# Retention and two feed-forward layers on one core: a new written order for the first stage, head-pair scores in alternating banks, attention inputs first

## The chip, the core and the metric

One of the eight cores of a Trainium2 chip runs the whole kernel. The metric is the time of one execution on the device, in microseconds (us). Its engines each take their own instructions in order: TensorE (PE in the profile, PEld for its weight loads), VectorE (DVE), ScalarE (ACT), GpSimd (POOL) and SyncE (SP), which here only issues transfers. Matrix results go to eight PSUM banks of 512 floats per partition, called bank 0 to 7 below.

## What is computed

```python
# q, k, v: (4, 8, 576, 64); every array is float32
scores = scale * q @ k.T
Dmat   = where(rel >= 0, gamma[head] ** rel, 0)     # rel = query position - key position
x      = (scores * Dmat) @ v                        # regrouped to 2304 tokens x 512
# layer 1, 512 -> 2048 -> 512, a cubic over a quadratic between its products
h = x @ w_in
g = (a0 + a1*h + a2*h**2 + a3*h**3) / (1 + |b0|*|h| + |b1|*h**2 + 1e-6)
x = g @ w_out
# layer 2, 512 -> 1536 -> 512
xn  = x / sqrt(mean(x*x) + 1e-6) * rms_g
out = (silu(xn @ w_gate) * (xn @ w_val)) @ w_out2
```

## The kernel before

**Attention** runs in 20 chunks, 4 batches of 5; a chunk has 128 positions, the last one of a batch 64. The decay between chunks is carried in a state `S` per head (64 by 64). The four head pairs of a chunk lie side by side in a bank, and the two heads of a pair lie in partitions 0 to 63 and 64 to 127 of the inputs.

**Layer 1** takes 384 tokens at a time (6 tiles) against 16 slices of `w_in` and `w_out`. One such pair of a tile and a slice is a step `s` of 96. Every float32 operand is split in a high and a low part, and three of the four products are made, so that a step has 12 matmuls up (`m1_up`) and 12 down (`m1_down`), of 384 columns each. The down products of a tile add up in banks 0 to 3 (`acc`). Weights arrive as float32 bits and are split by a chain over ACT, DVE and POOL (class `Weights`). **Layer 2** follows with its own weights.

**The first stage** is attention, the 32 weight slices of layer 1 and steps 0 to 17 of layer 1, all mixed. Its order is written out by hand: `PLAN` (L37) is a string of short names that are emitted one by one; `in_order` chains the instructions of each engine in that order, so every engine runs them as they stand and waits where an input is late. From step 18 on (`S0`) a plain loop takes over; the change doesn't touch it. The names that this text uses, with their engine:

| name | what it is | engine |
|---|---|---|
| LQ, LK | load of a chunk's q and k, of its k and v (`load_qk`, `load_kv`) | SP |
| LR | load of a weight slice (`Weights.load`), three buffers | SP |
| CH, CL, WH | weight split on ACT (L173, L180, L201) | ACT |
| CS, CG | weight split on DVE (L184, L191) | DVE |
| CA, WL | weight split, add (L197) and low part (L205) | DVE or POOL |
| PV | v times its decay (`prep_v`, L251) | POOL |
| SC | scores (`att_scores`, L263), one head of each pair, one bank | PE |
| R | scores times the mask (`att_mask`, L273), into one of three buffers | DVE |
| ST, SA | the chunk's own state (L341) and its addition to `S` (L350, L348) | PE, DVE |
| OS, OV | output from the state (L301) and from the chunk (L315) | PE |
| XO | output times its decay, into the one buffer `xe` (L324) | DVE |
| XS | store of `xe` to DRAM (L334) | SP |
| XH, XL | high and low part for the first token tile, chunks 0 to 2 | ACT, DVE |
| U, UU; D, DD | the halves of `m1_up` (L365 to L367); `m1_down` with g high (L374, L375) and low (L378) | PE |
| QQ | a product of the element-wise part (`el_qq`, L408) | POOL |
| PA, PB, NA, NB, NC, GL | other element-wise steps (L412, L416, L432, L436, L441, L451) | DVE |

A number behind a name is the chunk, the weight slice or the step `s`, and behind a slash stands the bank, or `v` and `p` for DVE and POOL. Ahead of `PLAN` five warming matmuls run on PE (L618), and ACT's queue issues the small tables.

Of the kernel before, what the change touches and what calls it, by code (L numbers as in the profile page):

```python
# [42 lines left out]
LQ7 LK7 PV5/p WH4 LR7 UU0 R11 CS5 SC12/4 CF0 BA0 CG5 BU0 CA5/v U1/6 BQ0 LR8 PV6/p PA0 WH5 UU1 R12 QQ0/p PB0
OV5/4 BA1 XO4 WL4/p BU1 SC13/7 LQ8 BQ1 XS4 PA1 PV7/p R13 YA0 YB0 PB1 ST5/7 QQ1/p CH6 SA5 LK8 NA0 CL7 SC14/7
WL5/p NB0 CL8 R14 CH7 CS6 OS6/7 YA1 NC0 YB1 CG6 OV6/0 GH0 NA1 PV8/p D0 LQ9 NB1 CS7 CA6/v LR9 CG7 WH6 GL0/v
WL6/p NC1 U2/5 XO5 GH1 CA7/p UU2 CH8 GL1/v XS5 LR10 CS8 ST6/4 WH7 CG8 SC15/6 LK9 BU2 SA6 CA8/p BA2 DD0 R15 BQ2
OS7/4 PA2 LR11 WL7/p CL9 PB2 SC16/6 WH8 XO6 QQ2/p CH9 OV7/0 R16 XS6 CL10 PV9/p U3/7 LQ10 YA2 CS9 YB2 ST7/6 CG9
CL11 UU3 LK10 SA7 CA9/p NA2 XR0 SC17/6 BA3 XR1 NB2 BU3 LR12 WL8/p D1 R17 BQ3 PA3 WH9 QQ3/p PB3 OS8/6 CH10 NC2
PV10/p OV8/0 YA3 XO7 YB3 CS10 U4/4 LQ11 GH2 CG10 XS7 NA3 CA10/p UU4 CL12 NB3 DD1 GL2/v BU4 LR13 WL9/p NC3
SC18/5 BA4 D2 GH3 R18 PA4 BQ4 PB4 CH11 SC19/5 QQ4/p GL3/v DD2 WH10 R19 ST8/7 YA4 CS11 WL10/p SC20/5 SA8 LK11  # L50
YB4 XO8 CL13 OS9/7 R20 CH12 XS8 U5/6 CG11 SC21/5 CA11/v LR14 CS12 WH11 OV9/0 CG12 UU5 LQ12 LK12 PV11/p NA4 D3
NB4 BA5 CA12/p BU5 R21 BQ5 PA5 OV10/5 LR15 WL11/p NC4 WH12 DD3 LQ13 PB5 CL14 QQ5/p XO10 CH13 SC22/5 XS10 GH4
# [5 lines left out]
WH17 U8/4 CG18 YA7 CA18/v UU8 YB7 LR21 WL17/p NA7 WH18 NB7 BA8 NC7 BU8 PV15/p GL6/v BQ8 WL18/p PA8 OS13/5 CH19
PB8 CL19 DD6 CS19 CH20 CG19 OV13/0 CL20 CS20 LQ16 QQ8/p XO12 GH7 CL21 GL7/v SC28/7 XS12 CA19/p D7 YA8 R28 YB8
LR22 CG20 WH19 U9/6 NA8 CA20/p NB8 SC29/7 NC8 UU9 WL19/p LR23 WH20 R29 GH8 XO13 ST13/7 CH21 WL20/p DD7 SA13  # L60
LK16 XS13 BA9 GL8/v SC30/5 BU9 CS21 CG21 OS14/7 BQ9 OV14/0 R30 CA21/p CH22 SC31/4 LQ17 PA9 CL22 LK17 PB9 U10/5
LR24 QQ9/p WH21 R31 CL23 PV16/p UU10 XO14 YA9 XS14 CS22 OV15/4 BU10 CG22 YB9 SC32/7 LQ18 PA10 CA22/p BA10 NA9
BQ10 D8 R32 LR25 PV17/p WH22 NB9 ST15/7 PB10 QQ10/p CL24 DD8 LK18 SA15 NC9 WL21/p SC33/7 YA10 XO15 YB10 R33
CH23 WL22/p OS16/4 XS15 GH9 NA10 OV16/0 CS23 CH24 CG23 U11/7 CL25 LQ19 CA23/v D9 LR26 CS24 WH23 CG24 NB10
PV18/p UU11 GL9/v CA24/p NC10 SC34/6 BU11 XO16 GH10 DD9 LR27 WL23/p PA11 WH24 XS16 SC35/4 R34 CL26 WL24/p PB11
ST16/6 CH25 SA16 LK19 BA11 R35 U12/6 BQ11 CS25 CH26 QQ11/p GL10/v U13/4 CL27 CG25 SC36/5 YA11 CS26 YB11 UU12
CA25/p R36 NA11 OS17/5 BU12 LR28 CG26 WH25 OV17/0 PV19/p PA12 BA12 PB12 UU13 BQ12 WL25/p NB11 NC11 D10 BU13
# [12 lines left out]
def retention_moe_kernel(  # L80
# [542 lines left out]
    act.activation(out=qb, in_=ones[:, 0:2], func=ACTF.Abs)  # L623
    act.dma_start(out=gv, in_=t_gv)
    act.dma_start(out=cf, in_=coef)
    act.dma_start(out=rg, in_=rms_g)
# [232 lines left out]
```

## Time and profile before

| what | value |
|---|---|
| median of three runs | 988.83 us (986.68 to 989.68) |
| the profiled execution, its own time | 990.85 us |
| its span, first to last instruction | 989.0 us |
| mean granted clock of TensorE | 0.989 |
| PE, PEld busy | 962.4 us (97%), 903.2 us (91%) |
| DVE, ACT, POOL busy | 569.8, 535.3, 325.0 us (58, 54, 33%) |

The profile and the trace are of that one execution; the 1.85 us between its time and its span lie outside the first and last instruction. Records of one engine overlap a little at their ends, and "busy" counts each moment once. A row ends with the idle time before it, and behind an arrow what ended that.

### The profile page before, as it was taken

The page shows a single profiled execution, that of the slowest core. Times are in us where ns is not written, and L with a number is a line of the kernel's source. Part 1 is how long each engine was busy: PE and PEld are TensorE (multiplying, and loading weights), DVE is VectorE, ACT ScalarE, POOL GpSimd, SP SyncE. Part 2 cuts the span into 40 slices and gives each one's busy share as a digit, 9 for nine tenths or more (in the row PEclk, how much of TensorE's full clock was granted, in tenths as well). Part 3 has the DMA queues.
Part 4 walks back from the last instruction along what each step waited for, and adds up shares of the span by engine and source line. Part 5 has one row for each costly group of instructions (what it writes and reads, how often), then busy time and mean ns, then how long its engine had stood idle before and what let it go on. Part 6 is the DMA issues. An engine that isn't in the chain of part 4 may idle for free. (4 is left out here: it accounts for less than half of the span.)

```text
span 989.0 us, 15086 instructions
## 1 busy us (share of the span) xinstructions
PE 962.4 (97%) x5854; PEld 903.2 (91%) x5854; DVE 569.8 (58%) x1022; ACT 535.3 (54%) x1028; POOL 325.0 (33%) x308
## 2 busy tenths in 40 slices
...
GB/s 352 280 239 239 222 271 121 105 1 33 33 1 43 22 32 33 1 33 33 22 75 96 107 155 131 125 112 95 34 1 64 1 1 49 1 1 19 14 1 32
DMA packets 38584, 79.85 MB, mean 81 GB/s; under 512 B 6256, under 2 KB 21744, under 8 KB 38512
## 3 DMA queue, kind: packets, MB, share of 16 engines
...
q8 instruction: 46, 0.75, 0.3%
...
## 5 line engine op out<-in xcount | busy, mean ns | idle before, releaser
L536 PE MATMUL bank<-x,w 128*128 128x384 f32 x528 | 176.8, 336 | 0.6 <-DVE sg L542 0.6
L537 PE MATMUL bank<-x,w 128*128 128x384 f32 x528 | 177.0, 335 | 0.3 <-POOL x L290 0.3
L538 PE MATMUL bank<-x,w 128*128 128x384 f32 x528 | 177.1, 335 | 0.0
L542 DVE TENSOR_TENSOR sg<-sg,bank 128x384 f32<-128x384 f32 x72 | 39.8, 553 | 217.8 <-PE bank L538 212.1
L290 POOL TENSOR_TENSOR x<-xr,x 128x384 fp32r<-128x384 f32 x44 | 47.7, 1099 | 287.1 <-ACT x L286 287.0
L365 PE MATMUL bank<-x,w 128*128 128x384 f32 x384 | 131.8, 343 | 6.9 <-DVE u L416 4.1
L374 PE MATMUL bank<-g,w 128*128 128x384 f32 x384 | 129.9, 340 | 3.0 <-ACT g L447 2.8
L367 PE MATMUL bank<-x,w 128*128 128x384 f32 x384 | 129.0, 336 | 0.0
L366 PE MATMUL bank<-x,w 128*128 128x384 f32 x384 | 128.9, 336 | 0.0
L375 PE MATMUL bank<-g,w 128*128 128x384 f32 x384 | 128.1, 335 | 0.1
L541 ACT ACTIVATE sg<-bank 128x384 f32<-128x384 f32 x72 | 35.4, 491 | 166.5 <-PE bank L538 166.5
L408 POOL TENSOR_TENSOR q<-q,ah 128x384 f32<-128x384 f32 x96 | 99.3, 1034 | 78.8 <-ACT q L395 75.7
L451 POOL TENSOR_TENSOR g<-u,g 128x384 fp32r<-128x384 f32 x80 | 82.3, 1029 | 69.0 <-issue 37.0
L536 PEld LDWEIGHTS bank<-x,w 128*128 128x128 f32 x528 | 99.1, 188 | 4.1 <-DVE sg L542 0.9
L537 PEld LDWEIGHTS bank<-x,w 128*128 128x128 f32 x528 | 99.1, 188 | 3.3 <-POOL x L290 0.7
L538 PEld LDWEIGHTS bank<-x,w 128*128 128x128 f32 x528 | 99.1, 188 | 0.4
L544 ACT ACTIVATE y<-sg 128x384 fp32r<-128x384 f32 x72 | 37.7, 524 | 101.8 <-DVE sg L542 101.8
L378 PE MATMUL bank<-g,w 128*128 128x384 f32 x384 | 86.8, 340 | 0.0
L412 DVE TENSOR_TENSOR u<-u,bank 128x384 f32<-128x384 f32 x96 | 52.9, 551 | 56.6 <-ACT u L401 53.5
L365 PEld LDWEIGHTS bank<-x,w 128*128 128x128 f32 x384 | 72.3, 188 | 11.6 <-DVE u L416 6.2
L374 PEld LDWEIGHTS bank<-g,w 128*128 128x128 f32 x384 | 72.3, 188 | 5.3 <-ACT g L447 4.1
L423 ACT ACTIVATE bank<-q,cst 128x384 f32<-128x384 f32 x96 | 56.0, 583 | 35.3 <-POOL q L408 28.1
...
## 6 DMA issues: line engine op xcount, KB each, us to landing
...
```

The source lines that it names most:

```text
L365: pe.matmul(out=h, lhsT=w[:, 0, ks], rhs=x[:, 0, k], start=(k == 0), stop=False)
L366: pe.matmul(out=h, lhsT=w[:, 0, ks], rhs=x[:, 1, k], start=False, stop=False)
L367: pe.matmul(out=h, lhsT=w[:, 1, ks], rhs=x[:, 0, k], start=False, stop=(k == KD - 1))
L374: pe.matmul(out=acc[m], lhsT=w[:, 0, ms], rhs=g[:, 0], start=(j == 0), stop=False)
L375: pe.matmul(out=acc[m], lhsT=w[:, 1, ms], rhs=g[:, 0], start=False, stop=False)
L378: pe.matmul(out=acc[m], lhsT=w[:, 0, ms], rhs=g[:, 1], start=False, stop=(j == J1 - 1))
L408: eng.tensor_tensor(out=q, in0=q, in1=el_t[i]["ah"], op=ALU.mult)
L423: act.activation(out=el[i], in_=el_t[i]["q"], func=ACTF.Abs_reciprocal_sqrt, bias=cst[:, 0:1])
L451: eng.tensor_tensor(out=g[:, 1], in0=el_t[i]["r"], in1=g[:, 0].bitcast(F32), op=ALU.subtract)
L536: pe.matmul(out=t, lhsT=w[:, 0, ks], rhs=x[:, 0, k], start=(k == 0), stop=False)
L537: pe.matmul(out=t, lhsT=w[:, 0, ks], rhs=x[:, 1, k], start=False, stop=False)
L538: pe.matmul(out=t, lhsT=w[:, 1, ks], rhs=x[:, 0, k], start=False, stop=(k == KD - 1))
```

## The change

- **A pair's scores.** `att_scores` makes both heads of a chunk in one go, into two banks, and takes the heads in turn: head 0 of pair 0, head 1 of pair 0, head 0 of pair 1, and so on. The two heads use different halves of the array's rows. A bank number over 99 gives two banks (`101` is banks 0 and 1).
- **Banks 0 to 3** serve attention too, as the order says; the first D stands behind the last chunk.
- **Masks.** The upper triangle comes into `ones` by a load and is set to 1 after the stage. A 64-position chunk takes one R over 128 partitions instead of two over 64, so there are 36 R instead of 40.
- **Tables.** The decay tables of chunks 1 to 4 of a batch were four loads on SP; now POOL makes them from the first (`make_gq`, 4 instructions). Two small tables go together in `ta`, two others in `cr`.
- **The order.** SP's first load is the first q and k instead of three weight slices. All of attention stands ahead of D0 and of U5; before, U14 stood ahead of the last chunk's outputs. Of the DVE and POOL work, counted in `PLAN`:

| name | before, DVE / POOL | now, DVE / POOL |
|---|---|---|
| PV | 0 / 20 | 9 / 11 |
| CA | 11 / 21 | 11 / 21 |
| WL | 7 / 25 | 13 / 19 |
| QQ | 0 / 18 | 6 / 12 |
| XL | 3 / 0 | 2 / 1 |
| R | 40 / 0 | 36 / 0 |
| GQ | 0 / 0 (four loads) | 0 / 4 |

```diff
 PLAN = """
-LR0 LR1 LR2 LQ0 LK0 LQ1 LK1 LQ2 LK2 GQ1 GQ2 GQ3 CH0 GQ4 CL0 CS0 CG0 CL1 CA0/v CH1 LR3 WH0 CS1 CG1 CL2 WL0/v
...
+LQ0 KC0 LK0 LR0 KG0 LQ1 LK1 LQ2 LK2 SC0/101 LR1 R0 LR2 PV0/p R1 ST0/0 CL0 OV0/1 SA0 CH0 GQ1 XO0 LQ3 GQ2 LK3
...
-    gv = at_p.tile([128, NC, NH, 1], F32, name="gv")
-    msk = at_p.tile([128, 1, CH], F32, name="msk")
+    ta = at_p.tile([128, HD + NC * NH + (NC - 1) * NP], F32, name="ta")
+    msk, msk_h = ones[:, None, :], ta[:, None, 0:HD]
...
-    def load_gq(c):
-        sp.dma_start(out=gq[c], in_=t_gq[c, :, :, 0:size(c)])
-
-    def att_scores(i, e, b):
-        n, ks = keys(i, e)
-        qk, r = qk_b[i % 3], slice(64 * e, 64 * e + 64)
-        sc = banks[b].rearrange("p (n c) -> p n c", n=NP)
+    def load_at():
+        sp.dma_start(out=ones, in_=t_dm)
+        sp.dma_start(out=ta, in_=t_at)
+
+    def make_gq(c):
+        n = size(c)
+        pool.tensor_tensor(
+            out=gq[c][:, :, 0:n], in0=gq[0][:, :, 0:n],
+            in1=gf[:, c - 1].to_broadcast([128, NP, n]), op=ALU.mult,
+        )
+
+    def att_scores(i, b):
+        qk = qk_b[i % 3]
+        for e in range(2):
+            rets[i, e] = banks[(b % 100 // 10 if b > 99 else b, b % 10)[e]].rearrange("p (n c) -> p n c", n=NP)
         for p in range(NP):
-            pe.matmul(
-                out=sc[ks, p, 0:n], lhsT=qk[r, 1, p, 0:n], rhs=qk[r, 0, p, 0:n],
-                start=True, stop=True,
-            )
-        rets[i, e] = sc
+            for e in range(2):
+                n, ks = keys(i, e)
+                r = slice(64 * e, 64 * e + 64)
+                pe.matmul(
+                    out=rets[i, e][ks, p, 0:n], lhsT=qk[r, 1, p, 0:n], rhs=qk[r, 0, p, 0:n],
+                    start=True, stop=True,
+                )
 
     def att_mask(i, e):
-        n, ks = keys(i, e)
+        n = size(steps[i][1])
         sc = rets[i, e]
         rets[i, e] = ret_p.tile([128, NP, CH], F32, tag="ret", name="ret")
+        if n < CH:
+            rets[i, 1] = rets[i, e]
         dve.tensor_tensor(
-            out=rets[i, e][ks, :, 0:n], in0=sc[ks, :, 0:n],
-            in1=msk[ks, :, ks].to_broadcast([n, NP, n]), op=ALU.mult,
+            out=rets[i, e][:, :, 0:n], in0=sc[:, :, 0:n],
+            in1=(msk if n == CH else msk_h).to_broadcast([128, NP, n]), op=ALU.mult,
         )
...
-        "SC": lambda i, a: att_scores(*divmod(i, 2), a),
+        "SC": att_scores,
...
-        "XL": lambda i, a: split_lo(0, *x0(i), dve),
+        "XL": lambda i, a: split_lo(0, *x0(i), a),
```

**The start, on SP.** These are its first transfers before (`raw` is a weight slice, `xb` q and k, `kv_...` k and v, `gq_...` a decay table):

```order
L163 DMA raw<-in_w_in_dram 128x1024 x3
L238 DMA xb<-in_qkT_dram 128x512 x2
L243 DMA kv_109<-in_kv_dram 128x1024
L238 DMA xb<-in_qkT_dram 128x1024
L243 DMA kv_110<-in_kv_dram 128x1024
```

and now:

```order
L237 DMA xb<-in_qkT_dram 128x1024
L255 DMA ones<-in_t_dm_dram 128x128
L256 DMA ta<-in_t_at_dram 128x120
L242 DMA kv_107<-in_kv_dram 128x1024
L163 DMA raw<-in_w_in_dram 128x1024
L649 DMA gq_110<-in_t_gq_dram 128x512
L237 DMA xb<-in_qkT_dram 128x1024
```

The first q and k are ahead of all else; the first weight slice is fifth, the second comes behind three chunks.

**The first scores, on PE.** Before (bank_98 is bank 0, bank_102 bank 4, and so on):

```order
L263 MATMUL bank_102<-xb 128x128 x4
L263 MATMUL bank_103<-xb 128x128 x4
L341 MATMUL bank_104<-kv_109 64x64 x8
L263 MATMUL bank_105<-xb 128x128 x4
L263 MATMUL bank_102<-xb 128x128 x4
L315 MATMUL bank_103<-ret,kv_109 64x128 x8
```

and now, from the third pair of the first chunk on (bank_97 is bank 0, bank_98 bank 1):

```order
L273 MATMUL bank_97<-xb 128x128
L273 MATMUL bank_98<-xb 128x128
L273 MATMUL bank_97<-xb 128x128
L273 MATMUL bank_98<-xb 128x128
L352 MATMUL bank_97<-kv_107 64x64 x8
L326 MATMUL bank_98<-ret,kv_107 64x128 x8
```

Four matmuls of one head in a row have become single ones of the two heads in turn, and the second chunk's scores, which stood ahead of the first chunk's output (L315), now stand behind it.

**The end of the stage, on DVE.** Bank 4 holds step 16, and step 18, the loop's first, waits for it. PB16 is the L416 row of bank_102 before; behind it stand GL14, GL15, PA17 and PB17:

```order
L441 SCALAR_TENSOR_TENSOR bank_104<-u,cf,bank_104 128x384
L416 SCALAR_TENSOR_TENSOR u<-u,cf,bank_102 128x384
L451 TENSOR_TENSOR g<-bank_105,g 128x384
L451 TENSOR_TENSOR g<-bank_104,g 128x384
L412 TENSOR_TENSOR u<-u,bank_103 128x384
L416 SCALAR_TENSOR_TENSOR u<-u,cf,bank_103 128x384
```

Now PB16 is the L427 row of bank_101, and PB17 that of bank_102:

```order
L427 SCALAR_TENSOR_TENSOR u<-u,cr,bank_101 128x384
L462 TENSOR_TENSOR g<-bank_103,g 128x384
L184 TENSOR_SCALAR ft<-ft 128x512
L191 SCALAR_TENSOR_TENSOR ft<-raw,ft 128x512
L443 SCALAR_TENSOR_TENSOR q<-q,bank_104 128x384
L447 SCALAR_TENSOR_TENSOR bank_104<-q,bank_104 128x384
L423 TENSOR_TENSOR u<-u,bank_102 128x384
L452 SCALAR_TENSOR_TENSOR bank_104<-u,cr,bank_104 128x384
L427 SCALAR_TENSOR_TENSOR u<-u,cr,bank_102 128x384
```

Between PB16 and PB17 there were three instructions and are now seven, two of them for the last weight slice. In `PLAN` ten DVE steps stand behind PB16 now, and four did before.

## Rows read from the trace of the kernel before

**Rows 1.** Busy time by stretch: us and instructions of each engine, clock, DMA share, GB/s.

```profile
0.00:187.84 187.84, 171.17 (x1555) 145.64 (x1555) 149.36 (x263) 117.00 (x211) 104.83 (x94) 0.95 0.72 234
9.95:187.84 177.89, 165.09 (x1545) 143.18 (x1545) 145.34 (x254) 111.87 (x203) 104.62 (x90) 0.95 0.72 231
187.84:500.00 312.16, 311.17 (x1771) 308.56 (x1772) 226.65 (x421) 247.76 (x498) 179.37 (x180) 0.99 0.09 28
```

**Rows 2.** Timeline of PE: the first matmul of step 18.

```profile
187.84 0.44 PE L365 MATMUL bank<-x,w 128*128 128x384 f32 x1 [2.62 <-DVE u L416]
```

**Rows 3.** Groups of DVE's instructions up to 187.8 us: busy us, mean ns, idle before.

```profile
L273 DVE TENSOR_TENSOR ret<-bank,msk 128x512 f32<-128x512 f32 x32 | 22.1, 689 | 12.0 <-PE bank L263 10.1 <-PE bank L315 1.6
L205 DVE TENSOR_TENSOR w<-ft,w 128x512 fp32r<-128x512 f32 x7 | 5.9, 854 | 0.0
L412 DVE TENSOR_TENSOR u<-u,bank 128x384 f32<-128x384 f32 x17 | 9.3, 549 | 3.3 <-ACT u L401 3.2
L273 DVE TENSOR_TENSOR ret<-bank,msk 64x256 f32<-64x256 f32 x8 | 3.4, 422 | 3.2 <-PE bank L263 3.2
L290 DVE TENSOR_TENSOR x<-xe,x 128x512 fp32r<-128x512 f32 x3 | 2.7, 906 | 0.1
```

**Rows 4.** The same for POOL.

```profile
L205 POOL TENSOR_TENSOR w<-ft,w 128x512 fp32r<-128x512 f32 x24 | 30.6, 1286 | 9.3 <-ACT w L201 9.2
L251 POOL TENSOR_TENSOR kv<-kv,gv 128x512 f32<-128x512 f32 x20 | 22.4, 1120 | 30.1 <-DMA kv<-in_kv_dram 28.4 <-PE bank L301 1.0 <-PE bank L263 0.7
```

**Rows 5.** Timeline of the first 12 us.

```profile
0.73 1.33 SPq L163 DMA_DIRECT2D raw<-in_w_in_dram  x3
1.45 6.08 PE L618 MATMUL bank<-xe 128*128 128x512 f32 x10 [1.45 <-DVE xe L614]
...
5.56 0.67 ACT L173 ACTIVATE ft<-raw 128x512 f32<-128x512 f32 x1 [2.41 <-DMA raw<-in_w_in_dram]
...
9.95 1.86 PE L263 MATMUL bank<-xb 64*128 64x128 f32 x16 [2.42 <-DMA xb<-in_qkT_dram]
...
11.15 1.40 DVE L273 TENSOR_TENSOR ret<-bank,msk 128x512 f32<-128x512 f32 x2 [0.44 <-PE bank L263]
```

**Rows 6.** Timeline of PE in attention at the full clock.

```profile
19.33 1.16 PE L263 MATMUL bank<-xb 64*128 64x128 f32 x8
20.41 0.69 PE L341 MATMUL bank<-kv 128*64 128x64 f32 x16
20.93 1.05 PE L315 MATMUL bank<-ret,kv 128*64 128x128 f32 x16
21.90 1.09 PE L301 MATMUL bank<-xb,S 64*64 64x128 f32 x16
...
26.49 1.71 PE L263 MATMUL bank<-xb 64*128 64x128 f32 x16
```

**Rows 7.** Timeline of PE in attention at half the clock.

```profile
45.39 1.99 PE L263 MATMUL bank<-xb 64*128 64x128 f32 x8 [0.53 <-DVE S L348]
48.16 1.97 PE L301 MATMUL bank<-xb,S 64*64 64x128 f32 x16 [0.78 <-DVE ret L273]
50.06 1.97 PE L315 MATMUL bank<-ret,kv 128*64 128x128 f32 x16
```

**Rows 8.** Busy time by stretch, as in rows 1: around falls of the clock, and a gap without one.

```profile
42.15:45.56 3.41, 2.10 (x29) 1.68 (x26) 2.27 (x5) 3.35 (x6) 3.23 (x4) 0.99 0.85 299
45.56:52.39 6.83, 6.05 (x41) 5.09 (x42) 5.98 (x11) 3.70 (x8) 1.04 (x1) 0.50 0.39 116
158.20:161.60 3.40, 2.11 (x28) 1.78 (x28) 2.60 (x6) 1.93 (x4) 3.01 (x3) 0.99 0.65 175
110.00:120.00 10.00, 7.44 (x66) 6.39 (x65) 9.49 (x18) 8.48 (x16) 6.61 (x6) 1.00 0.58 175
```

**Rows 9.** Transfers of the stage: count, KB, median us to landing.

```profile
x_d<-xe SPq DMA_DIRECT2D x13, 256.0 KB, 3.9
```

**Rows 10.** Busy time by stretch: layer 1 alone, and the end of the stage.

```profile
153.60:181.46 27.86, 25.23 (x215) 23.11 (x213) 24.00 (x41) 20.02 (x39) 15.79 (x15) 0.94 0.41 118
200.00:225.00 25.00, 25.00 (x144) 24.73 (x143) 17.63 (x34) 19.51 (x38) 14.70 (x16) 1.00 0.00 1
```

More of the change, by code (lines that the diff above doesn't have):

```diff
@@ L43 @@
[L43 to L52, printed above, removed]
@@ L58 @@
[L58 to L67, printed above, removed]
@@ L73 @@
-YB14 CS30 CL31 WL29/v UU16 BA15 CG30 BQ15 D13 NA14 CA30/p CH31 NB14 BU16 NC14 QQ15/p UU17 WH30 PA16 GH14
-WL30/v DD13 YA15 CS31 D14 YB15 CG31 BU17 NA15 CA31/p BA16 NB15 BQ16 NC15 WH31 QQ16/p PB16 GH15 GL14/v WL31/p
-BA17 GL15/v DD14 BQ17 PA17 YA16 QQ17/p PB17 YB16
+LQ0 KC0 LK0 LR0 KG0 LQ1 LK1 LQ2 LK2 SC0/101 LR1 R0 LR2 PV0/p R1 ST0/0 CL0 OV0/1 SA0 CH0 GQ1 XO0 LQ3 GQ2 LK3
+SC1/102 XH0 GQ3 OS1/1 R2 GQ4 R3 SC2/102 XL0/v PV1/v R4 PV2/p ST1/3 OV1/0 SA1 CS0 CH1 CG0 ST2/0 LQ4 CL1 LK4
+OS2/3 R5 CA0/p CL2 XO1 OV2/0 SA2 XH1 LR3 CS1 WH0 XL1/v SC3/101 LQ5 LK5 WL0/v OS3/2 XO2 PV3/p CH2 R6 XH2 ST3/3
@@ new lines @@
+PA2 U3/5 PV9/p LQ10 CH6 R17 LK10 PB2 UU3 QQ2/p CL7 CS5 OS8/0 YA2 CS6 XR0 CG5 BA3 XR1 YB2 ST8/2 XO7 BU3 CA5/p
+OV8/0 NA2 XS7 BQ3 PA3 SC9/1 QQ3/p WH5 LR8 NB2 LQ11 SA8 SC10/134 LK11 R18 WL5/p NC2 OS9/1 PB3 GH2 OV9/0 PV10/p
+R20 CH7 U4/6 YA3 GL2/v LK12 LQ12 R21 YB3 ST10/2 CG6 CL8 UU4 CS7 SA10 CA6/p XO8 OV10/2 NA3 BA4 XS8 WH6 CG7 LR9
+SC11/103 BU4 LQ13 NB3 WL6/p LK13 BQ4 NC3 OS11/4 PA4 GH3 PV11/p R22 CH8 PB4 QQ4/p ST11/0 R23 PV12/v YA4
+SC12/137 YB4 GL3/v CA7/p XO9 OV11/0 R24 XS9 WH7 LR10 SA11 ST12/1 NA4 LQ14 CL9 LK14 OS12/0 CS8 NB4 R25 SC13/135
@@ new lines @@
+NC4 PV13/v OV12/0 XO10 ST13/7 SA12 XS10 CG8 LK15 CL10 OS13/1 LQ15 R26 CA8/p R27 SC14/2 SA13 WH8 LR11 OV13/0
+WL7/v R28 WL8/p CH9 OS14/3 XO11 LK16 LQ16 XS11 PV14/v CH10 PV15/v OV14/0 CS10 ST15/2 LK17 CS9 LQ17 SC15/145
+CG10 SA15 CG9 CL11 R30 CA9/p R31 OV15/2 CA10/v WH9 LR12 PV16/v WH10 LR13 SC16/145 LK18 WL9/v LQ18 WL10/p XO12
+CH11 ST16/7 R32 XS12 OS16/0 R33 CS11 OV16/0 SA16 CG11 SC17/145 PV17/v LQ19 LK19 CA11/p ST17/7 CL12 R34 CH12
+R35 OS17/4 LR14 WH11 CS12 CL13 WL11/v OV17/0 SA17 CH13 PV18/p CS13 ST18/5 CG12 OS18/7 CG13 CA12/v SA18 CA13/p
@@ new lines @@
+WH12 LR15 XO13 OS19/5 XS13 WL12/v WH13 LR16 PV19/v CH14 WL13/v CL14 CS14 CG14 CH15 CL15 CA14/p XO14 XS14
+SC18/113 CS15 WH14 LR17 CG15 CL16 R36 WL14/p R37 SC19/1 CA15/p CH16 XO15 OV18/0 R38 XS15 OV19/0 CS16 WH15 LR18
+CG16 CL17 WL15/v XA0 XA1 XB0/p CH17 XB1/p XR2 XO16 XS16 D0 CA16/v XR3 CL18 CS17 LR19 WH16 CG17 DD0 WL16/v XA2
+D1 CA17/v GH4 CH18 XB2/p GL4/v LR20 WH17 XO17 DD1 XA3 CS18 XS17 U5/4 WL17/v CG18 CL19 UU5 XB3/p CH19 U6/6
+CA18/v CL20 BU5 CS19 LR21 XO18 UU6 WH18 CG19 BA5 XS18 BQ5 WL18/v D2 BA6 CA19/v BU6 PA5 QQ5/p LR22 WH19 U7/7
@@ new lines @@
+GL8/v YB10 NC9 D7 BU11 NA10 CH25 CG24 GH9 NB10 U12/5 CA24/p CL26 GL9/v BA11 PA11 UU12 BQ11 CS25 LR27 PB11 WH24
+QQ11/p NC10 DD7 BA12 BU12 WL24/v D8 GH10 CG25 CH26 PA12 YA11 U13/4 CS26 BQ12 CA25/v CL27 CG26 UU13 LR28 WH25
+QQ12/v YB11 CA26/v DD8 BA13 GL10/v WL25/p WH26 LR29 D9 NA11 BQ13 PB12 BU13 WL26/p NB11 CH27 U14/6 PA13 YA12
+NC11 QQ13/p CH28 PB13 UU14 CL28 CS27 YA13 CS28 DD9 CG27 CL29 YB13 D10 CG28 YB12 NA13 CA27/p GH11 NA12 BU14
+DD10 GL11/v BA14 CA28/p LR30 NB12 WH27 D11 NB13 BQ14 NC12 WL27/p LR31 WH28 PA14 GH12 DD11 NC13 WL28/p CH29
@@ L76 @@
+PB14 U15/7 GH13 GL12/v GL13/v CH30 UU15 QQ14/v CL30 CS29 YA14 CS30 U16/4 CG29 BU15 YB14 CG30 D12 CL31 CA29/v
+BA15 NA14 CA30/p WH29 PA15 UU16 BQ15 NB14 WL29/p WH30 PB15 U17/5 BU16 NC14 BA16 QQ15/v UU17 CH31 PA16 WL30/p
+GH14 PB16 YA15 DD12 GL14/v BA17 CS31 YB15 D13 BQ16 CG31 BU17 NA15 QQ16/p BQ17 NB15 DD13 PA17 CA31/p YA16 D14
+NC15 YB16 PB17 GH15 QQ17/p WH31 GL15/v DD14 WL31/v
 """
@@ L236, in load_qk @@
     def load_qk(i):
-        for a in (slice(0, 1), slice(1, 2)) if i == 0 else (slice(0, 2),):
-            sp.dma_start(out=qk_b[i % 3][:, a], in_=qkT[steps[i]][:, a])
+        sp.dma_start(out=qk_b[i % 3], in_=qkT[steps[i]])
     def load_kv(i):
```

59 lines of the change are left out of this document (28 added, 31 removed).

## Prediction

> **What bounds the kernel now.** I read the busy time by stretch first, to find the stage in which the change can act. Step 18, the first that the plain loop issues, starts on PE at 187.84 us [rows 2]. From there PE is busy 311.17 of the next 312.16 us [rows 1], and nothing there is changed: what the end gains is what that start gains. So the question is how early step 18 starts.
>
> Up to there PE is busy 165.09 us of the 177.89 since its first score, 92.8% [rows 1]. DVE comes next with 149.36 us, then ACT with 117.0 and POOL with 104.8 [rows 1]. PE bounds the stage, and DVE, at some 82%, waits mostly for it: the masks alone waited 12.0 + 3.2 us, nearly all for scores [rows 3]. The wait that ends last ahead of step 18 is one for DVE: 2.62 us until PB16 (L416) frees bank 4 [rows 2].
>
> **The change part by part.**
>
> *Scores.* Sixteen score records of one chunk take 1.71 us [rows 6]. The sixteen of OS, whose two heads alternate in two quarters of the array, take 1.09 with as many columns each [rows 6], so work on different parts of the array runs at once. The two heads of a chunk's scores use different halves of the rows; I take 1.09 us for an alternating pair, between 1.0 (OV, 1.05) and 1.71 (no overlap). With the switches between forms each half now costs about 1.08 us from start to start (20.41 less 19.33 [rows 6]), so a full chunk saves about 1.0 us of PE and one of 64 positions about 0.6: 16 x 1.0 + 4 x 0.6 = 18 us of PE. PE would need 147 us; it no longer bounds the stage if DVE needs more.
>
> *DVE.* It takes over 9 PV, 6 WL and 6 QQ and gives up one XL and half of the eight half masks. WL: 6 x 0.854 = 5.1. QQ, an operation as L412: 6 x 0.549 = 3.3. XL: -0.9. Masks: -4 x 0.422 = -1.7 [rows 3]. PV on DVE has no row; a product of 512 columns costs 0.689 with one operand in PSUM (L273) and 0.854 with both in SBUF (L205), and POOL's other work can stretch it as it did XL (0.906) [rows 3]. I take 0.75, since WL has the same form, POOL is less loaded now and records overlap a little: 6.8, with 6.2 and 8.2 as ends. Sum: +12.6 us. POOL loses 9 x 1.12 and 6 x 1.286 [rows 4] and six QQ, and gains four tables of a similar size; it bounds nothing either way.
>
> So the stage passes from PE to DVE: 147 against about 162 us. Less the opening memsets (0.7, which lie ahead of the first score), and less 3.5 us because ten steps instead of four now stand behind PB16 (by the rows of 0.55 to 0.69 us for such steps, 5.8 against 2.3), DVE has 149.4 + 12.6 - 0.7 - 3.5 = 157.8 us between its first mask and PB16.
>
> *The start.* A single 512 KB load issued at 0.73 us was used at 5.56; the first scores waited for theirs until 9.95, behind three weight slices [rows 5]. Now q and k go first and the warming matmuls, which end at 7.53 [rows 5], decide: first score 7.4, first mask 1.2 later as before (11.15 less 9.95), at 8.6. That is 2.5 us gained. The weight slice that ACT had at 5.56 comes three transfers later, some 3 us; attention covers that, since the first U stands behind four chunks.
>
> *How full DVE can be.* This decides the result, and no row shows it. Lower end: the 82% that it had while it waited for PE; step 18 would then start at 8.6 + 192 = 201 us and the kernel be 15 us slower, but 18 us of PE's work, the reason of most of those waits, are gone. Upper end: 9.49 of 10 us in its fullest stretch shown [rows 8]. The nearest row for an engine that bounds this stage and whose order was laid out around it is PE's 92.8% [rows 1]; I take 92%: 157.8 / 0.92 = 171.5 us, so PB16 ends and step 18 starts at 180.1, 7.7 us earlier.
>
> *The end of the stage.* Step 19 waits for PB17, which now stands seven instructions behind PB16 (4.6 us by those rows), while PE has step 18 and DD14 to do (16 matmuls at 25.00 / 144 = 0.174 us, 2.8 us [rows 10]). I charge 1.5 us of the 1.8; at worst all of it, at best nothing if DVE has caught up.
>
> *The store chain.* `xe` is one buffer, so an XO waits for the store of the one before: 0.69 + 3.9 us [rows 9] = 4.6 per chunk. Counted by rows, DVE has 93 us of work up to XO16, 5.5 for each of 17 chunks, which covers that on the whole; but between XO13 and XO16 the written order has 9.8 us of DVE work for three such waits of 13.8: about 3 us stand open there, and they are in the 8% that DVE idles.
>
> *Sum* against the profiled execution: 990.85 - 7.7 + 1.5 = 984.6 us. The median is 2.0 us under that execution, so the forecast is **982.5 us**.
>
> [...] By the estimate above an alternating pair of scores takes 1.09 us, while its two masks take 2 x 0.689 = 1.38 [rows 3], so the readers are slower than the writers.
> [...]
>
> **The rivals.**
>
> 1. *ACT and DVE hold each other up after attention.* From D0 to PB16 the order has about 65 us of DVE and 67 of ACT (counts times rows), PE only 53: two engines are near full at once and feed each other step by step. For it: at the end of the stage before, where the mix is much the same, DVE reached only 24.0 of 27.86 us, 86%, with PE at 25.2 [rows 10]. Against: the last chunks and some time at half clock lie in that stretch (0.94). At 86%, 65 / 0.86 - 65 / 0.92 = 5 us are lost: **987.5**, within 0.3% (3 us, about what a measurement of this kernel can tell from no change).
>
> 2. *The scores don't overlap*, so the change doesn't do what it says. PE then saves only switches, some 4 us, and needs 161 beside DVE's 158. With both that near to full I expect DVE at 88 to 90%: step 18 between 187.9 and 183.9 us, so a loss of 1.5 to a gain of 2.4 with the wait behind it: **988**. Against it speaks OS [rows 6], for it only that its tiles are quarters and these are halves.
>
> 3. *The clock falls in attention, and PE is the bound again; slower.* The clock stood at half after stretches of attention in which PE was busy 2.10 of 3.41 and 2.11 of 3.40 us, then stayed there for 6.83 us although PE was busy 6.05 of them; around a gap of layer 1, with 7.44 of 10 us, it did not fall [rows 8]. At half clock OS and OV take 1.97 us each and half a chunk's scores 1.99 [rows 7], so a chunk needs about 7.2 us of PE (scores 2.1, ST 1.2, OS and OV 2.0 each) against 3.7 at full clock. From SC11 to OV17 the order gives DVE 29.7 us for seven chunks, 4.2 each; with PE at 3.7 and waits between, it is filled as those stretches were. Each chunk at half clock costs 3.0 us. Two of them eat the gain, from the fourth on the kernel is slower by over 0.3%; with five it is 982.5 + 15 = **997.5**. [...]
> [...]
>
> **How the numbers follow.** The forecast, DVE at 90 to 95%: at 95% it is 157.8 / 0.95 = 166.1, step 18 at 174.7, no wait behind it and the cheaper PV, 975; at 90% 986. Chance 0.62, all of it faster. Rival 1 has 0.14 and rival 2 0.08, both within 0.3%. Rival 3 has 0.16, slower. The range, 973 to 995, holds the forecast's own (975 to 986) and some way below it for a DVE fuller still, rivals 1 and 2 whole and the milder part of rival 3 (up to four chunks); it leaves out the rest of rival 3 and the 82% above.
>
> **What would show it right or wrong.** Right: the sixteen score records of a chunk in about 1.1 us; the first score near 7.4 us; step 18 near 180 us; DVE busy over 90% up to there, PE under 85%, and masks that hardly wait for scores. Rival 1: DVE full in attention and under 88% behind it, waiting for ACT. Rival 2: 1.7 us for a chunk's scores. Rival 3: a granted clock under 0.9 between some 50 and 100 us, and masks that wait for scores at half speed. The forecast is wrong if step 18 starts before 173 or after 185 us, or if the time behind step 18 (801 us to the end) changes by over 2 us, which no step above explains.

## The result, and the profile after

The changed kernel takes **978.17 us** (median of four runs, 975.19 to 979.91); the kernel before took 989.25 in the runs beside it (four, 986.68 to 991.60). The ratio is 0.9888, with a 95% interval of 0.9859 to 0.9916: faster by some 11 us. The forecast was 982.5 with a range of 973 to 995. The profiled execution is the fastest of the four, 975.19 us, with a span of 973.4.

Busy time by stretch answers to [rows 1, 8] (us; busy us and instructions of PE, PEld, DVE, ACT and POOL; clock, DMA share, GB/s). The first three lines are the stage, the stage from the first mask on, and the start of the plain loop; then the stage's attention part and its layer-1 part; then a gap and the fall of the clock behind it:

```profile
0.00:171.68 171.68, 148.07 (x1555) 129.44 (x1556) 149.81 (x275) 112.61 (x209) 90.42 (x77) 0.96 0.74 251
9.29:171.68 162.39, 140.27 (x1529) 125.86 (x1530) 149.30 (x272) 110.83 (x207) 89.17 (x72) 0.96 0.74 250
171.68:500.00 328.32, 324.20 (x1847) 319.68 (x1847) 243.83 (x450) 260.54 (x525) 186.76 (x186) 1.00 0.09 30
9.29:104.52 95.23, 78.25 (x1196) 66.85 (x1196) 86.21 (x158) 50.40 (x88) 50.34 (x42) 0.95 0.94 330
104.52:171.68 67.16, 62.02 (x333) 59.02 (x334) 63.09 (x115) 60.43 (x119) 38.83 (x31) 0.97 0.44 137
91.20:94.60 3.40, 1.10 (x18) 0.87 (x18) 2.56 (x5) 1.55 (x4) 0.66 (x1) 0.99 0.90 269
94.60:108.20 13.60, 9.82 (x73) 8.89 (x74) 12.16 (x19) 7.82 (x14) 7.06 (x6) 0.50 0.70 200
```

DVE is busy 149.30 of 162.39 us, 91.9%, and PE 140.27, 86%. Before it was PE with 92.8% and DVE with some 82% [rows 1]. Step 18 starts at 171.68 instead of 187.84 [rows 2], 16.2 us earlier, and from there to the end of the span 801.7 us pass, against 801.2 before: the whole gain lies in the stage. (These are the two profiled executions; the medians lie only 11 us apart.)

PE's timeline at the start, at the fall of the clock and at the end of the stage (start, us; L273 are the scores, L376 a first matmul of m1_up, L385 of m1_down) answers to [rows 2, 6, 7]:

```profile
8.09 1.16 PE L273 MATMUL bank<-xb 64*128 64x128 f32 x16
10.08 0.69 PE L352 MATMUL bank<-kv 128*64 128x64 f32 x16 [0.82 <-issue]
10.63 1.09 PE L326 MATMUL bank<-ret,kv 128*64 128x128 f32 x16
11.65 1.16 PE L273 MATMUL bank<-xb 64*128 64x128 f32 x16
12.74 1.09 PE L312 MATMUL bank<-xb,S 64*64 64x128 f32 x16
...
96.23 2.07 PE L273 MATMUL bank<-xb 64*128 64x128 f32 x14 [3.56 <-DVE xe L335]
98.85 1.12 PE L273 MATMUL bank<-xb 64*64 64x64 f32 x16 [0.55 <-DVE ret L284]
99.90 3.02 PE L326 MATMUL bank<-ret,kv 128*64 128x128 f32 x32
104.52 0.69 PE L385 MATMUL bank<-g,w 128*128 128x384 f32 x1 [1.60 <-DVE xe L335]
...
171.68 0.33 PE L376 MATMUL bank<-x,w 128*128 128x384 f32 x1
...
174.81 0.44 PE L376 MATMUL bank<-x,w 128*128 128x384 f32 x1 [0.19 <-DVE u L427]
```

Sixteen scores take 1.16 us, where they took 1.71 [rows 6]. Step 18 finds its bank free, and step 19 waits 0.19 us. The one long wait of PE in attention, 3.56 us, is for a bank that an XO (L335) had not read yet, and the clock falls to half within it (0.50 from 94.6 us on).

Ahead of step 18 PE waits not for PB16 (the L427 row) but, in the two D before it, for a WL on POOL (L205) and for g's high part on ACT (L458):

```profile
167.72 0.44 PE L386 MATMUL bank<-g,w 128*128 128x384 f32 x1 [1.00 <-POOL w L205]
...
169.38 0.61 DVE L427 SCALAR_TENSOR_TENSOR u<-u,cr,bank 128x384 f32<-128x384 f32 x1
170.16 0.44 PE L385 MATMUL bank<-g,w 128*128 128x384 f32 x1 [0.25 <-ACT g L458]
```

PB16 ends at 169.99 us and frees bank 4 some 1.7 us before PE comes to step 18. Up to there DVE is busy 147.79 of 160.70 us since the first mask, 92.0%.

The start, from the timeline, answers to [rows 5]:

```profile
0.74 0.40 SPq L237 DMA_DIRECT2D xb<-in_qkT_dram  x1
...
1.45 6.71 PE L628 MATMUL bank<-xe 128*128 128x512 f32 x10 [1.45 <-DVE cst L630]
...
8.99 0.67 ACT L180 ACTIVATE raw<-raw 128x512 int32<-128x512 uint32 x1 [6.33 <-DMA raw<-in_w_in_dram]
9.29 0.69 DVE L284 TENSOR_TENSOR ret<-bank,ones 128x512 f32<-128x512 f32 x1 [7.87 <-PE bank L273]
```

The warming matmuls end at 8.16 us and the first score stands right behind them. DVE's groups up to step 18 (busy us, mean ns, idle before) answer to [rows 3]; L284 are the masks, L250 is PV and L419 QQ:

```profile
L191 DVE SCALAR_TENSOR_TENSOR ft<-raw,ft 128x512 int32<-128x512 int32 x32 | 24.7, 778 | 0.2
L284 DVE TENSOR_TENSOR ret<-bank,ones 128x512 f32<-128x512 f32 x32 | 21.2, 683 | 8.8 <-PE bank L273 8.7
L184 DVE TENSOR_SCALAR ft<-ft 128x512 int32<-128x512 int32 x32 | 16.0, 507 | 1.9 <-ACT ft L173 1.7
L335 DVE TENSOR_TENSOR xe<-bank,gq 128x512 f32<-128x512 f32 x16 | 10.9, 684 | 3.2 <-DMA x_d<-xe 2.6 <-PE bank L326 0.5
L205 DVE TENSOR_TENSOR w<-ft,w 128x512 fp32r<-128x512 f32 x12 | 8.4, 697 | 0.1
L250 DVE TENSOR_TENSOR kv<-kv,ta 128x512 f32<-128x512 f32 x9 | 6.2, 689 | 0.3 <-DMA kv<-in_kv_dram 0.3
L419 DVE TENSOR_TENSOR q<-q,ah 128x384 f32<-128x384 f32 x6 | 3.5, 581 | 0.2 <-ACT q L406 0.2
```

Of the masks' 8.7 us of waiting, 7.87 are the wait for the first score. A WL on DVE takes 0.697 us, where the seven before took 0.854.

### The profile page after: what moved, and what is told of

It is laid out like the page before. It is cut to its first block, busy times and chain, and to the rows that moved or that the text cites. A ratio compares the mean times of both kernels' runs of the same rounds, so it can differ in the third digit from the quotient of the medians.

```text
span 973.4 us, 15053 instructions
## 1 busy us (share of the span) xinstructions
PE 938.6 (96%) x5854; PEld 885.2 (91%) x5854; DVE 573.0 (59%) x1038; ACT 531.1 (55%) x1028; POOL 309.7 (32%) x292
## 5 line engine op out<-in xcount | busy, mean ns | idle before, releaser
L376 PE MATMUL bank<-x,w 128*128 128x384 f32 x384 | 130.7, 340 | 5.3 <-DVE g L462 3.4
L385 PE MATMUL bank<-g,w 128*128 128x384 f32 x384 | 130.2, 341 | 5.7 <-ACT g L458 3.5
L419 POOL TENSOR_TENSOR q<-q,ah 128x384 f32<-128x384 f32 x90 | 93.7, 1042 | 82.0 <-ACT q L406 78.6
L376 PEld LDWEIGHTS bank<-x,w 128*128 128x128 f32 x384 | 72.1, 188 | 10.0 <-DVE u L427 4.1
L385 PEld LDWEIGHTS bank<-g,w 128*128 128x128 f32 x384 | 72.5, 189 | 8.1 <-ACT g L458 4.9
```

The lines of the kernel that those rows point to most:

```text
L376: pe.matmul(out=h, lhsT=w[:, 0, ks], rhs=x[:, 0, k], start=(k == 0), stop=False)
L385: pe.matmul(out=acc[m], lhsT=w[:, 0, ms], rhs=g[:, 0], start=(j == 0), stop=False)
L419: eng.tensor_tensor(out=q, in0=q, in1=el_t[i]["ah"], op=ALU.mult)
```

## Experiments

My theory at this point: PE bounded the stage before; its cheaper scores take it off the bound, and DVE sets the pace now. The rivals were that the alternation is the gain whatever DVE does, that the new order and division give it whatever the scores cost, and that transfers (DMA share 0.94 in attention) set the pace. The kernel before ran beside every experiment, so ratios are compared below; executions of one kernel lie 1 to 9 us apart.

**Heads in turn, off.**

```diff
-        for p in range(NP):
-            for e in range(2):
+        for e in range(2):
+            for p in range(NP):
```

> The changed kernel, with the two heads of a chunk's scores no longer in turn: all four pairs of head 0, then all four of head 1, in the same two banks and the same order of everything else. My theory: DVE is what fills the stage now (149.3 of the 162.4 us from the first mask to step 18) and PE has some 22 us of slack, so a chunk's scores go back from 1.16 to about 1.7 us, PE's work in the stage grows by about 10 us (148 to 158), and most of it lies beside DVE: step 18 starts 0 to 6 us later, I take 4, and the kernel takes about 979 to 984 us. Rival A, PE's saving is itself the gain: the full 10 to 13 us come back, 988 to 991. Rival B, PE doesn't matter at all: within 1 us.

Measured: 979.05 us, ratio 0.9883 (0.9845 to 0.9920), not to be told from the changed kernel. PE's work did grow by what was expected, 9.6 us. These are the scores alone on PE, from the first one to step 18; first the kernel before:

```profile
9.95:187.84 177.89, 42.48 (x320) 35.73 (x320) 0.95 0.72 231
```

then this experiment, and all engines of it in the same stretch:

```profile
7.89:173.29 165.40, 33.23 (x320) 29.40 (x320) 0.96 0.74 248
...
7.89:173.29 165.40, 151.03 (x1546) 136.96 (x1545) 147.72 (x272) 111.52 (x207) 89.20 (x73) 0.96 0.74 248
```

then the changed kernel:

```profile
8.09:171.68 163.59, 23.57 (x320) 19.54 (x320) 0.96 0.74 251
...
8.09:171.68 163.59, 141.44 (x1546) 126.83 (x1546) 149.31 (x272) 111.12 (x207) 89.68 (x73) 0.96 0.74 251
```

The change saves 18.9 us of scores on PE. Half of it, 9.2 us, comes without the alternation, with both heads of a chunk made in one go; the other half, 9.7 us, is the alternation. Time at half clock has little part in this: in the stretches at full clock one score record takes 127, 100 and 70 ns in the three kernels. Removing the alternation costs the kernel nothing that can be told from no change (0.9 us by the medians, and by the ratios it is 0.05 points faster). Rival A falls: PE at 151 us is already off the bound. My own 4 us did not come either; what came is rival B, within 1 us.

**Fewer scores in the kernel before**, the cut of PE without the new order.

```diff
-        for p in range(NP):
+        for p in range(NP if i < 4 else NP // 2):
```

> The kernel before, with the score matmuls of head pairs 2 and 3 left out from chunk 4 on (half of those chunks' scores are not computed; the masks still read whole banks). This takes about 12 us of PE out of the old order, nearly what the alternation takes out, and changes nothing else. My theory, PE bounds the stage before: 8 to 10 us less, 979 to 981. Rival, the new order and the new division of work give the gain and a cheaper score alone is hardly worth anything in the old order (its waits are for DVE and transfers at fixed places): 3 us less or under, 986 or more.

Measured: 981.00 us, ratio 0.9906 (0.9872 to 0.9941). All engines from the first score to step 18:

```profile
9.68:177.34 167.66, 149.43 (x1417) 127.58 (x1417) 146.66 (x254) 111.48 (x203) 104.58 (x90) 0.97 0.74 245
```

PE lost 15.7 us (165.09 to 149.43; part of it is less time at half clock, the mean granted clock being 0.97 against 0.95) and step 18 came 10.5 us earlier. So PE did bound the old stage, and with PE near 150 us that order gives nearly the whole gain. In the old order, then, 165 us of PE were too much, and in the new one 151 still don't matter; where between the two PE begins to matter, in either order, no run tells. Nor does any run have the new order with the scores at their old cost, so how much the order would give by itself stays open.

**The same load on DVE, in three places.** Twenty memsets behind the XO of the changed kernel, the same in the kernel before, and thirteen wider ones behind PB5 to PB17 of the changed kernel:

```diff
             out=xe[:, :, 0:n], in0=ob_t[i][:, :, 0:n], in1=gq[c][:, :, 0:n], op=ALU.mult
         )
+        dve.memset(spare, 0.0)
...
             out=u, in0=u, scalar=cf[:, 1:2], in1=el[i], op0=ALU.subtract, op1=ALU.mult
         )
+        if 5 <= i < S0:
+            dve.memset(spare, 0.0)
```

> The changed kernel with one more instruction on DVE behind each of the 20 XO: a memset of a spare 128x512 tile that nothing reads, some 0.49 us each by the memset rows, 9.7 us in all, all of it in the attention part. My theory, DVE sets the pace from the first mask on: 8 to 10 us more, 986 to 988. Rival, the transfers set it up to 95 us (their share stands at 0.92 to 1.02 there, and the late start of the weights-first run was made up): DVE has 7.6 us of idle time up to 95 us, which takes most of the memsets: 1 to 4 us more, 979 to 982.

> The kernel before, with the same 20 memsets behind its XO that the changed kernel was given (9.7 us of DVE). My theory, PE bounds the stage before and DVE has slack at 82%: 0 to 4 us more, less than the 3.7 us by which the changed kernel's median rose. Rival, DVE's fixed places in the order matter in the old order just as much as in the new one: 4 to 8 us more.

> The changed kernel with a memset of 128x768 on DVE (some 0.72 us by the 0.485 of 512 columns) behind PB5 to PB17, 12 of them ahead of step 18: 8.6 us, all in layer 1's part of the stage, from some 110 us on, where DVE is busy 94 to 96%. Theory, DVE sets the pace there though it didn't fully in attention (9.7 us there cost 3.7): 6 to 8.5 us more, 984 to 987. Rival, ACT (90 to 93% there) or PE (92%) sets it as much: 2 to 4 us more.

Measured: behind the XO of the changed kernel 981.90 us, ratio 0.9931 (0.9908 to 0.9955); in the kernel before 991.66, ratio 1.0009 (0.9984 to 1.0033); in layer 1's part 985.45, ratio 0.9971 (0.9948 to 0.9995). Against the unloaded kernels that is 0.43, 0.09 and 0.83 points, or some 4, 1 and 8 us; the first is just clear of the noise. The run with the late load, in its two parts (D0 starts at 105.12 us here):

```profile
7.49:105.12 97.63, 80.22 (x1213) 68.53 (x1212) 86.30 (x158) 50.53 (x88) 50.18 (x43) 0.95 0.94 330
105.12:179.94 74.82, 62.27 (x325) 59.21 (x326) 69.65 (x124) 60.59 (x117) 39.68 (x31) 0.95 0.40 124
```

DVE's busy time in the second part rose from 63.09 to 69.65 us, and the part itself from 67.16 to 74.82, 7.7 us for memsets of 8.4. So **in layer 1's part DVE sets the pace, nearly one to one** (the memsets also hold up the element-wise steps behind them; with DVE idle for only 4.1 of 67.16 us there, the two can hardly be told apart); of the load behind the XO less than half reaches the end; in the kernel before next to none did. My expectation for the load behind the XO, 8 to 10 us, was too high, and its rival's 979 to 982 came: the memsets of 9.7 us lengthened DVE's busy time by 7.4 (149.31 to 156.68 from the first score to step 18), and the stretch by 4.2 (163.59 to 167.75); the rest filled gaps of DVE, 14.3 us of them before and 11.1 after. Seventeen of the twenty memsets stand ahead of D0, and from the first score to D0 the stretch grew only from 96.43 to 98.25 us; in the run with the late load, which has none there, it is 97.63:

```profile
7.79:175.54 167.75, 144.70 (x1546) 129.45 (x1545) 156.68 (x293) 111.14 (x207) 91.73 (x73) 0.95 0.73 246
```

**The division between DVE and POOL.** First PV alone back on POOL; then, in the new order, QQ too and the WL as they were in the kernel before. The entries of `PLAN` that change (first pair: in both; second: in the second alone):

```diff
-PV1/v PV5/v PV12/v PV13/v PV14/v PV15/v PV16/v PV17/v PV19/v
+PV1/p PV5/p PV12/p PV13/p PV14/p PV15/p PV16/p PV17/p PV19/p
...
-QQ6/v QQ8/v QQ9/v QQ12/v QQ14/v QQ15/v WL1/v WL7/v WL9/v WL11/v WL12/v WL13/v WL15/v WL17/v WL18/v WL24/v WL31/v
-WL14/p WL27/p WL28/p WL29/p WL30/p
+QQ6/p QQ8/p QQ9/p QQ12/p QQ14/p QQ15/p WL1/p WL7/p WL9/p WL11/p WL12/p WL13/p WL15/p WL17/p WL18/p WL24/p WL31/p
+WL14/v WL27/v WL28/v WL29/v WL30/v
```

> The changed kernel with all 20 PV on POOL, as in the kernel before (9 moved back, DVE loses 9 x 0.69 = 6.2 us, POOL gains 9 x 1.12 = 10). Theory, DVE sets the pace: up to 6 us less, 972 to 976, unless POOL's slower PV comes late for ST and OV. Rival, transfers set the pace in attention, where the PV are: within 1 us, or 1 to 3 us more because a PV on POOL stands behind longer instructions and holds ST, OV and then the v buffer's next load.

> The changed kernel's order with the kernel before's division between DVE and POOL: all PV and QQ on POOL, and the WL on DVE that were there before (7 instead of 13). DVE loses 9 PV, 6 QQ and 6 WL, some 6.2 + 3.3 + 4.2 = 13.7 us, POOL gains 10 + 5 + 7.7, some 23, to 113 us of the stage's 172. Theory, the division is part of the gain because POOL's forms of the same work are slower and late: 2 to 5 us more, 980 to 983. Rival A, DVE alone sets the pace: 6 to 12 us less, 966 to 972. Rival B, the order alone gives the gain: within 1.5 us.

Measured: 976.75 us, ratio 0.9895 (0.9865 to 0.9925), no difference, so my 972 to 976 can't be told from its rival; and 982.54 us, ratio 0.9941 (0.9913 to 0.9970), about 5 us slower. In the second, DVE's stage and groups read:

```profile
7.55:177.19 169.64, 143.64 (x1546) 128.22 (x1545) 149.12 (x252) 112.15 (x208) 111.83 (x94) 0.95 0.72 244
...
L191 DVE SCALAR_TENSOR_TENSOR ft<-raw,ft 128x512 int32<-128x512 int32 x32 | 29.5, 929 | 0.3
L184 DVE TENSOR_SCALAR ft<-ft 128x512 int32<-128x512 int32 x32 | 21.8, 692 | 5.8 <-ACT ft L173 5.7
L284 DVE TENSOR_TENSOR ret<-bank,ones 128x512 f32<-128x512 f32 x32 | 21.3, 682 | 8.8 <-PE bank L273 8.8
...
L205 DVE TENSOR_TENSOR w<-ft,w 128x512 fp32r<-128x512 f32 x7 | 7.5, 1077 | 0.2 <-ACT w L201 0.2
```

DVE has 20 instructions fewer and is busy just as long, 149.12 us: what it gave away came back in the length of those that stayed. The 6 us by which the stage is longer are idle time of DVE (20.5 against 14.3 us); it waits more for the weight split on ACT (L184, 5.7 against 1.7) and for stores of `xe` (5.5 against 2.9). By the ratios the new order with the old division keeps 0.59 of the 1.12 points, so about half of the gain needs the new division. Groups between SBUF tiles grew (L191 778 to 929 ns, L184 507 to 692, L205 697 to 1077); the masks, which read PSUM, kept 682. That could still be due to which instructions stand side by side, so one more run added POOL work only.

**A load on POOL.**

```diff
             out=xe[:, :, 0:n], in0=ob_t[i][:, :, 0:n], in1=gq[c][:, :, 0:n], op=ALU.mult
         )
+        pool.tensor_tensor(out=spare, in0=spare, in1=spare, op=ALU.mult)
```

> The changed kernel with one more product of 128x512 on POOL behind each XO (of a spare tile that nothing else reads, the size of a PV: 1.1 us each, 22 us in all; POOL is busy 90 of 172 us). My theory, work on POOL lengthens DVE's instructions between SBUF tiles (with the old division DVE's L191 took 929 instead of 778 ns, L184 692 instead of 507, L205 1077 instead of 697, while those that read PSUM kept their length): those groups grow by some 10 to 25%, DVE is busy 6 to 10 us longer though it gets no instruction, and the kernel takes 3 to 6 us more, 981 to 984. Rival, the lengthening with the old division came from which instructions stand beside each other: DVE's groups keep their length and the kernel its time, within 1 us, since POOL has 80 us to spare.

Measured: 982.44 us, ratio 0.9920 (0.9896 to 0.9945), some 3 to 4 us slower; the intervals overlap, so what counts here is DVE's busy time. The stage, and DVE's groups up to 176 us (lines are one or two on):

```profile
8.20:178.72 170.52, 141.42 (x1546) 125.30 (x1545) 158.49 (x272) 111.61 (x207) 113.05 (x93) 0.97 0.72 241
...
L192 DVE SCALAR_TENSOR_TENSOR ft<-raw,ft 128x512 int32<-128x512 int32 x31 | 26.0, 846 | 0.2
L285 DVE TENSOR_TENSOR ret<-bank,ones 128x512 f32<-128x512 f32 x32 | 21.1, 681 | 9.5 <-PE bank L274 9.5
L185 DVE TENSOR_SCALAR ft<-ft 128x512 int32<-128x512 int32 x31 | 18.5, 605 | 1.4 <-ACT ft L174 1.4
...
L206 DVE TENSOR_TENSOR w<-ft,w 128x512 fp32r<-128x512 f32 x12 | 10.0, 834 | 0.0
...
L251 DVE TENSOR_TENSOR kv<-kv,ta 128x512 f32<-128x512 f32 x9 | 7.9, 886 | 0.0
```

POOL got 23.4 us of work (89.68 to 113.05) and DVE, with the same 272 instructions, is busy 9.2 us longer (149.31 to 158.49). PV on DVE went from 689 to 886 ns, the masks stayed at 681. This is more than the runs differ by without such a load: in the four with the changed kernel's division (heads in turn off, two store buffers, weights first, loads cut) DVE's 272 instructions are busy 146.88 to 149.46 us, and L191, L184, WL and PV take at most 761, 550, 768 and 792 ns. The rival falls: POOL's work costs DVE time, here 0.4 us for each us, in groups that work between SBUF tiles, though not in all of them.
L197, which reads two SBUF tiles like L191, WL and PV, does not show it: 933 ns in the changed kernel, 943 with the load and 851 with the old division. L184, which reads one, does: 507, 605 and 692 ns. What sets L197 apart was not shown. In the kernel before, the three XL of [rows 3] took 0.69, 0.68 and 1.35 us; only the third, from 29.97 to 31.32 us, ran beside an instruction of POOL, a PV from 29.73 to 30.77.

**Stores, loads and the start.** Two output buffers in turn instead of one (the store and the first token tile's splits take the same buffer); no k loaded for the chunk's own state from chunk 3 on; the three first weight slices ahead of the first q and k (the start of the first line of `PLAN`); and the two buffers together with PV on POOL:

```diff
-            out=xe[:, :, 0:n], in0=ob_t[i][:, :, 0:n], in1=gq[c][:, :, 0:n], op=ALU.mult
+            out=xe2[i % 2][:, :, 0:n], in0=ob_t[i][:, :, 0:n], in1=gq[c][:, :, 0:n], op=ALU.mult
...
-            sp.dma_start(out=kv_b[i % 3], in_=kv[steps[i]])
+            h = slice(0 if i < 3 else 1, 2)
+            sp.dma_start(out=kv_b[i % 3][:, h], in_=kv[steps[i]][:, h])
...
-LQ0 KC0 LK0 LR0 KG0 LQ1 LK1 LQ2 LK2 SC0/101 LR1 R0 LR2 PV0/p R1
+LR0 LR1 LR2 LQ0 KC0 LK0 KG0 LQ1 LK1 LQ2 LK2 SC0/101 R0 PV0/p R1
```

> The changed kernel with two buffers for the attention output on its way to DRAM, taken in turn, instead of one; no instruction is added or moved. In the changed kernel DVE waits 2.9 us in six places for the store of the chunk before, and PE waits 3.6 and 1.6 us for a bank that such an output holds, after which the clock is at half for 13.6 us. My theory, the store chain costs the stage what these waits say and the fall of the clock goes with them: 3 to 5 us less, 973 to 975. Rival, DVE and PE wait at the next place instead (the order is fixed, and the stores share the queues with the loads): 0 to 1 us less, 977 to 978.

> The changed kernel without the load of k for the chunk's own state from chunk 3 on (the state is made from an old k): 13 loads get 256 KB smaller, 3.4 MB in all of the some 29 MB that move up to 95 us, about 10 us of transfer time at the 345 GB/s seen there. No instruction of an engine is removed. Theory, DVE sets the pace: within 1 us, 977 to 979. Rival, the transfers set the pace in attention: 4 to 9 us less, 969 to 974, with step 18 as much earlier.

> The changed kernel with the three first weight slices loaded ahead of the first q and k, as in the kernel before; nothing else is changed. My theory: the first score comes at about 10.6 us instead of 8.1, and since DVE is 92% full from there, all of it arrives at the end: 2.5 to 3 us more, 980.5 to 981.5. Rival, the stage makes up the late start because something behind it (loads, the store chain) sets the pace: 0 to 1 us more.

> The changed kernel with two store buffers and all PV on POOL together; each alone gave some 1 us by the medians, which the measurement hardly tells from nothing. With PV on POOL DVE waited 5.8 us for stores (2.9 in the changed kernel), which the second buffer removes. Theory, the two removed waits complete each other: 3 to 5 us less than the changed kernel, 973 to 975. Rival, the stage is near even between PE, DVE and the transfers, and nothing that relieves one is worth much: 976 to 978.

Measured, in this order: 977.02 us, ratio 0.9860 (0.9824 to 0.9897); 975.76, ratio 0.9879 (0.9856 to 0.9902); 978.81, ratio 0.9873 (0.9829 to 0.9918); 977.17, ratio 0.9861 (0.9823 to 0.9899). None can be told from the changed kernel, so none is a better version that the measurement shows. For the buffers, and for them with PV on POOL, my 973 to 975 did not come; the rivals' figures did. In the changed kernel DVE's waits included

```profile
DVE ret L284 <- PE bank L273: 9.1, 5, 7.9
...
DVE xe L335 <- DMA x_d<-xe: 2.9, 6, 1.2
```

(us, times, longest), and with two buffers the second of these is gone and the first is longer, as are others:

```profile
DVE ret L285 <- PE bank L274: 11.0, 6, 7.6
DVE q L444 <- ACT bank L440: 3.1, 3, 1.5
```

An 11% cut of the attention part's transfers (3.4 MB of the 31 that 330 GB/s give in 95.23 us), some 10 us of transfer time at that rate, was worth 1 us by the ratio, 2.4 by the median: the transfers alone don't set the pace, though the profile can't exclude that they cost a little. What sets the pace in attention stays open. From the first score to D0 the changed kernel takes 96.43 us; with 9.6 us more of PE (heads in turn off) it is 98.78, with seventeen memsets on DVE 98.25, with the transfers cut 94.45, and runs with no load in that part lie up to 98.18 (two store buffers). The weights-first run missed its premise: its first score came at 8.28 us, not 10.6, so it doesn't tell what a late start costs. Why the kernel before waited until 9.95 [rows 5] behind the same three slices stays open; its first q and k were two loads, and SP waited 2.5 us for another transfer ahead of the second, where the weights-first run issued one load at 2.13 us.

## Why the prediction was right, and where it was off

- **Bound and sign: right.** PE bounded the stage (fewer scores alone gave 0.9906), and now DVE does in layer 1's part, at least (8 us for twelve memsets of 0.70). One sign was missed: PE is busy 86% of the stage from the first mask on, not under 85%.
- **Scores: right.** 1.16 us for an alternating pair against 1.09, 18.9 us of PE against 18. What I did not see is that half of it is not the alternation's, and that the second half is worth nothing that can be measured here, since 151 us are enough. By my step too, DVE decides as soon as PE is below it; I put no number on how much of the 18 us that took.
The prediction set two masks, 1.38 us, against an alternating pair of scores, 1.09; found were 2 x 0.683 = 1.37 and 1.16 us, so the readers are the slower here too. But apart from the start the masks waited for scores by only 0.8 us, and the full masks are 21.2 of DVE's 149.3 busy us, so these readers alone don't account for a second half that is worth nothing measurable.
- **How full DVE can be: right, in part by luck.** 92% taken, 92.0% found between the first mask and PB16's end. The value was PE's old share, for want of a nearer row; with the old division the same order filled DVE to 149.12 of 169.64 us, 88%.
- **DVE's work: the term that was mis-sized.** 157.8 us predicted between the first mask and PB16, 147.8 found (the 149.30 above run on to step 18). The step that failed took 12.6 us for the moved instructions at their rows' means, on top of the busy time of before, and left all other rows as they were. Two things were wrong in it. First, many instructions were shorter: a WL took 0.697 us, not 0.854, a PV 0.689, not 0.75, and L184 507 instead of 549 ns. The groups' own busy times add up to 163.9 us up to PB16, where the prediction's terms give 169.9 (161.5 before, plus 12.6, less 0.7 and 3.5). Second, those sums are not busy time, since records overlap at their ends: they exceed it by 16.1 us now and by 12.1 before (161.5 against 149.4). By this some 6 of the 10 us are the first and 4 the second, which is worked out, not tested. Whether the first came from POOL's smaller load stays open, too. The run with the load shows that POOL's work can set this length (L184 507 to 605 ns); but L191 grew while POOL's work fell, and L184's 549 lies within what the four runs named there spread over, 472 to 550. In the kernel before the two read:

```profile
L191 DVE SCALAR_TENSOR_TENSOR ft<-raw,ft 128x512 int32<-128x512 int32 x32 | 23.9, 748 | 0.7
L184 DVE TENSOR_SCALAR ft<-ft 128x512 int32<-128x512 int32 x32 | 17.6, 549 | 6.1 <-ACT ft L173 5.8
```

- **The start**: 9.29 us for the first mask, not 8.6; the warming matmuls took 6.71 us, not the 6.08 of [rows 5].
- **Step 18 and the wait behind it**: 171.68 instead of 180.1, 0.19 instead of 1.5 us. By the prediction's own line, a start before 173 us, the sum was wrong there, and in the direction of more gain. With 147.8 in DVE's term it would have given 8.6 + 160.7 = 169.3 for step 18 and 973.8 us for the profiled execution, which took 975.19. The path was wrong, too, in its last wait: PB16 was done at 169.99, and PE came to step 18 1.7 us behind it, after the waits for POOL and ACT. That, the start (0.7 us late) and the wait behind step 18 (1.3 us less) nearly make up the rest. The medians, 989.25 and 978.17, show 11 us, since the two profiled executions lay apart from their medians in opposite directions.
- **The store chain: right as an idle of DVE** (2.9 us of waits against 3). My later expectation that a second buffer would gain it was wrong: with that buffer the wait stood elsewhere.
- **The tail: right**, 801.7 against 801.2 us.
- **Rival 1** did not come: in layer 1's part DVE is busy 63.09 of 67.16 us, 94%, beside ACT with 90%. **Rival 2** neither: 1.16 us. **Rival 3** came in small: one fall of the clock, at the end of attention (94.6 to 108.2 us, with PE busy 9.82 of the 13.60), after 3.4 us in which PE was busy 1.10. Between 50 and 100 us the granted clock is 0.95, not under 0.9. No run here tells what the fall cost.
